# Values of two head pairs in one PSUM group, a lighter TensorE convolution in half the channel groups, and a planner that knows tiling switches

## The chip, the cores and the metric

One core of a Trainium2 chip runs the whole program. The metric is the device time of one execution in microseconds (us). "TensorE" or PE is the matmul engine, "VectorE" or DVE and "ScalarE" or ACT the two engines that read its results from PSUM here, POOL is GpSimd, SP issues the transfers.

## The reference

Banded attention (window of 32 to each side) for 8 batches, 8 heads, 576 positions and 64 channels a head; its output, as 576 x 512 per batch, goes through a gated FFN with a depthwise convolution of three taps.

```python
scores = np.where(abs(pos[:, None] - pos[None, :]) <= 32, q @ k.T / 8, -1e9)
x = softmax(scores) @ v                       # 8 x 576 x 512
h = np.maximum(x @ w_in, 0.0)                 # 8 x 576 x 1024
conv = sum(conv_w[k] * shifted(h, k - 1) for k in range(3))
out = (h * sigmoid(conv)) @ w_out             # 8 x 576 x 512
```

## The kernel before

The program declares each piece of work with its engine, an assumed duration and a priority. A planner (`place`) then fixes the order of all instructions and the PSUM banks (8 of 512 fp32 columns; bank pairs start at even banks). So an edit can move everything. The FFN runs in 12 blocks of 384 positions, each with 8 channel groups of 128. Attention for a later batch is woven between.

The convolution of one channel group: PE applies taps by multiplying with diagonal matrices, in blocks 0 and 1 all three, later only the outer two. VectorE then adds the middle tap in PSUM, ScalarE takes tanh, VectorE gates.

```python
def TAPS(c):
    return (0, 1, 2) if c < 2 else (0, 2)
...                                            # cut: in hidden(), for each group m
for kk in TAPS(c):
    nc.tensor.matmul(ps(sl, 0, no), diag_w[:, kk, m, :], hview(m, o0, o1, kk - 1),
                     start=(kk == 0), stop=(kk == 2))
...
if len(TAPS(c)) == 2:
    nc.vector.scalar_tensor_tensor(out=pv(), in0=mid, scalar=conv_w_sb[:, 1, m:m + 1],
                                   in1=pv(), op0=ALU.mult, op1=ALU.add)
```

The values step: for one pair of heads, 8 or 12 small matmuls (128x64 tiling of the array, 65 columns: 64 of values, one of row sums) into one bank, one reciprocal of the row sums, one multiply.

```python
def values(b, s, g, t):                        # cut
    sl = Slot(1)                               # one bank
    ...                                        # 4 * n matmuls of 64x65
    nc.vector.reciprocal(rv, view()[:, :, :, D])
    nc.vector.tensor_tensor(out=xn[...], in0=view()[:, :, :, 0:D], in1=rv..., op=ALU.mult)
...
for g in range(NP):                            # 4 pairs of heads
    values(b, s, g, ...)
```

Scores are in a third tiling (64x128), so PE's order switches between three modes. The planner before takes no account of that.

The softmax here doesn't subtract the row's maximum and nothing guards it: scores larger than these inputs give would overflow.

## Time and profile before

| | before |
|---|---|
| time, median of 4 runs | 237.56 us (236.97 to 238.3) |
| span of the profiled execution | 235.7 us |
| busy: PE, DVE, ACT, POOL | 94%, 72%, 76%, 66% |
| first matmul of FFN block 2, from the span's start | 62.6 us |
| from there to the end of PE's work ("the stretch") | 169.4 us |
| priced PE work in the stretch / PE standing still | 166.4 / 3.1 us |

The last rows come from PE's matmul starts in the trace.

### The profile page before, as it was taken

How to read it: one execution, taken by the hardware profiler on the slowest of the kernel's cores; microseconds unless marked ns; L12 is line 12 of the kernel's file. 1: busy time of each engine (PE TensorE's matmuls, PEld its weight loads, DVE VectorE, ACT ScalarE, POOL GpSimd, SP SyncE). 2: the span in 40 equal slices, each digit the busy share in tenths (PEclk: the TensorE clock that was granted, in tenths of full speed). 3: DMA queues.
4: the chain of work that ended last, by engine and by line, in shares of the span. 5: the costliest groups of instructions: out<-in, count | busy, mean ns of one | idle time of the engine just before them, and what ended most of it. 6: DMA issues, size and time to landing. Idle time of an engine off the chain costs nothing.

```text
span 235.7 us, 6684 instructions
## 1 busy us (share of the span) xinstructions
PE 222.7 (94%) x2556; PEld 134.6 (57%) x2556; DVE 169.1 (72%) x405; ACT 179.3 (76%) x360; POOL 154.8 (66%) x153
## 2 busy tenths in 40 slices
PE   3897999899989999999999999999999999999993
PEld 1455798758656555555565555655554655555541
DVE  7557777649599667867795957967887858956570
ACT  4689898959868877787969687888868876666652
POOL 3367885999999769697879669797988670000000
PEclk9999999999999999999999999999999999999999
DMA  5999999998875659997796969879989311421113
GB/s 161 248 334 322 274 281 284 315 263 272 202 179 148 172 152 263 236 168 211 202 216 168 293 163 261 244 185 243 240 246 155 87 56 44 104 89 44 65 71 133
DMA packets 68884, 45.93 MB, mean 195 GB/s; under 512 B 53980, under 2 KB 54004, under 8 KB 68852
## 3 DMA queue, kind: packets, MB, share of 16 engines
q1 hardware_dynamic: 68816, 45.50, 73.1%
q8 instruction: 20, 0.33, 0.6%
q14 instruction: 12, 0.10, 0.1%
q10 hardware_dynamic: 36, 0.01, 0.0%
HBM read 32.52 MB, written 9.44 MB: 178 GB/s over the span
## 4 chain that ended last, share of the span: by engine, by line
PE 65%; DMA 13%; SPq 6%; POOL 5%; DVE 3%; issue 3%; ACT 2%; ACTq 0%; POOLq 0%
PE ps_all L771 21%; PE ps_all L699 21%; PE ps_all L729 11%; DMA vst<-in_v_dram 7%; PE ps_all L570 5%; PE ps_all L478 4%; DMA wst<-in_moe_w_out_dram 4%; PE ps_all L528 3%; SPq L378 3%; DMA kst<-in_k_dram 2%; SPq L409 2%; SPq L601 1%; POOL vo L290 1%; POOL ve L290 1%; POOL w_out_sb L290 1%
## 5 line engine op out<-in xcount | busy, mean ns | idle before, releaser
L699 PE MATMUL ps_all<-xT,w_in_sb 128*128 128x385 bf16 (+4 forms) x448 | 78.6, 304 | 1.2 <-ACT xT L288 0.7
L771 PE MATMUL ps_all<-w_out_sb,gT 128*128 128x512 bf16 x288 | 67.4, 379 | 0.0
L751 DVE SCALAR_TENSOR_TENSOR gT<-ps_all,hT 128x384 bf16<-128x384 f32 (+3 forms) x112 | 53.8, 493 | 15.7 <-ACT ps_all L748 14.8
L744 DVE SCALAR_TENSOR_TENSOR ps_all<-hT,conv_w_sb,ps_all 128x384 f32<-128x384 bf16 x80 | 48.6, 616 | 20.1 <-PE ps_all L729 19.6
L552 POOL TENSOR_TENSOR attn<-attn,mask 128x1024 bf16<-128x1024 bf16 x24 | 50.8, 2133 | 12.0 <-ACT attn L541 11.1
L715 ACT ACTIVATE hT<-ps_all 128x385 bf16<-128x385 f32 (+4 forms) x112 | 49.7, 459 | 10.1 <-PE ps_all L699 9.5
L748 ACT ACTIVATE ps_all<-ps_all 128x384 f32<-128x384 f32 (+3 forms) x112 | 48.7, 450 | 10.5 <-DVE ps_all L744 8.4
L699 PEld LDWEIGHTS <-w_in_sb 128*128 128x128 bf16 x448 | 40.2, 98 | 21.7 <-issue 1.2
L729 PE MATMUL ps_all<-hT,diag_w 128*128 128x384 bf16 (+3 forms) x256 | 50.9, 297 | 0.2 <-ACT attn L541 0.2
L771 PEld LDWEIGHTS <-gT 128*128 128x128 bf16 x288 | 27.3, 98 | 29.5
L782 ACT COPY y<-ps_all 128x512 f32<-128x512 f32 x36 | 21.1, 590 | 24.9 <-PE ps_all L771 20.6
L541 ACT ACTIVATE attn<-ps_all 128x1024 bf16<-128x1024 f32 (+1 forms) x40 | 36.7, 943 | 0.3 <-PE ps_all L528 0.2
L290 POOL TENSOR_SCALAR vo<-vst 64x1024 bf16<-64x1024 f32 (+1 forms) x34 | 33.0, 971 | 4.0 <-DMA vst<-in_v_dram 1.4
L590 DVE TENSOR_TENSOR xn<-ps_all,rec 128x256 bf16<-128x256 f32 (+1 forms) x64 | 29.1, 484 | 0.3
L290 POOL TENSOR_SCALAR ve<-vst 128x512 bf16<-128x512 f32 (+1 forms) x39 | 24.3, 631 | 4.6 <-DMA vst<-in_v_dram 3.8
L290 POOL TENSOR_SCALAR kn<-kst 128x1152 bf16<-128x1152 f32 (+1 forms) x19 | 19.2, 1012 | 11.9 <-DMA kst<-in_k_dram 8.5
L729 PEld LDWEIGHTS <-diag_w 128*128 128x128 bf16 x256 | 21.2, 97 | 9.8 <-issue 0.3
L552 DVE TENSOR_TENSOR attn<-attn,mask 128x1024 bf16<-128x1024 bf16 (+1 forms) x16 | 15.0, 944 | 8.9 <-ACT attn L541 8.8
L570 PEld LDWEIGHTS <-attn 128*64 128x64 bf16 x640 | 13.3, 111 | 11.6 <-issue 9.2
L290 POOL TENSOR_SCALAR qn<-qst 128x1152 bf16<-128x1152 f32 (+1 forms) x18 | 18.7, 1045 | 0.7 <-PE ps_all L699 0.2
L570 PE MATMUL ps_all<-ve,attn 128*64 128x65 bf16 x384 | 17.4, 197 | 0.8 <-ACT hT L715 0.7
L288 ACT COPY qT<-ps_all 128x640 bf16<-128x640 bf16 (+1 forms) x24 | 17.4, 754 | 0.3
(50 smaller groups left out, 174.1 us busy)
## 6 DMA issues: line engine op xcount, KB each, us to landing
qst<-in_q_dram SPq DMA_DIRECT2D x32, 288.0 KB, 5.0
kst<-in_k_dram SPq DMA_DIRECT2D x32, 288.0 KB, 5.2
out_dram<-y SPq DMA_DIRECT2D x36, 256.0 KB, 3.0
vst<-in_v_dram SPq DMA_DIRECT2D x23, 256.0 KB, 6.1
vst<-in_v_dram SPq DMA_DIRECT2D x16, 192.0 KB, 5.6
wst<-in_moe_w_in_dram SPq DMA_DIRECT2D x2, 1024.0 KB, 7.6
wst<-in_moe_w_out_dram SPq DMA_DIRECT2D x2, 1024.0 KB, 8.9
xT<-xn SPq DMA_TRANSPOSE x30, 2.7
```

Source lines behind the costliest of these rows:

```text
L290: nc.gpsimd.tensor_scalar(out=out_, in0=in_, scalar1=1.0, scalar2=0.0, op0=ALU.mult, op1=ALU.add)
L541: add(act(2 * w), t + 0.1, lambda e: nc.scalar.activation(at, ps(sl, 0, 1024).rearrange("p (e x) -> p e x", e=2)[:, :, 0:w], AF.Exp, bias= ...
L552: lambda e: ENG[e].tensor_tensor(out=x_, in0=x_, in1=m_, op=ALU.mult),
L570: nc.tensor.matmul(ps(sl, (D + 1) * (n * h_ + x), (D + 1) * (n * h_ + x + 1), 64 * j, 64 * j + 64), attn[a][:, 512 * h_ + col:512 * h_ + c ...
L590: add(dve(2 * n * D), t + 0.1, lambda e: nc.vector.tensor_tensor(out=xn[i][:, cs[0]:cs[0] + n].rearrange("p c (e g) d -> p c e g d", e=2)[ ...
L699: nc.tensor.matmul(ps(sl, 0, n), w_in_sb[:, kc, m * 128:(m + 1) * 128], x_[:, kc, a0:a1], start=(kc == 0), stop=(kc == KC - 1),)
L715: nc.scalar.activation(o_, i_, AF.Relu, bias=0.0, scale=0.5)
L729: nc.tensor.matmul(ps(sl, 0, no), diag_w[:, kk, m, :], hview(m, o0, o1, kk - 1), start=(kk == 0), stop=(kk == 2),)
L744: add(("DVE", no / 960.0 + 0.13), tt + 0.1, lambda e, m=m, mid=mid, pv=pv: nc.vector.scalar_tensor_tensor(out=pv(), in0=mid, scalar=conv_w ...
L748: add(act(no), tt + 0.2, lambda e, sl=sl: nc.scalar.activation(ps(sl, 0, no), ps(sl, 0, no), AF.Tanh, bias=0.0, scale=1.0), writes=[sl], s ...
L751: add(dve(no), tt + 0.3, lambda e, m=m, mid=mid, i2=i2, pv=pv: nc.vector.scalar_tensor_tensor(out=gT[ig][:, m, o0:o1].rearrange("p (i x) - ...
L771: nc.tensor.matmul(ps(sl, 0, d_model), gT[ig][:, m, 128 * i:128 * i + 128], w_out_sb[:, m, :], start=(m == 0), stop=(m == MB - 1),)
```

## The change

The intent is to take work from PE, which is solid after the opening. Four channel groups of eight ("light") leave only the middle tap to PE, from block 2 on, and VectorE adds both outer taps. Values of two head pairs go through one two-bank group with one reciprocal. The planner charges 0.105 us for a switch of tiling and prefers to stay in a mode. All its times were tuned anew. Cut to its core:

```diff
-    def TAPS(c):
-        return (0, 1, 2) if c < 2 else (0, 2)
+    def taps(c, m):
+        if c < 2:
+            return TIMES["taps"][c]                       # (0, 1, 2)
+        return (1,) if m in TIMES["light"] else (0, 2)    # light: 1, 2, 3, 7
...
-            if len(TAPS(c)) == 2:
-                add(("DVE", no / 960.0 + 0.13), ...)      # middle tap
+            for kk in (0, 1, 2):
+                if kk in taps(c, m):
+                    continue
+                add(("DVE", no / 960.0 + 0.13), ...)      # each tap that PE left out
...
-    def values(b, s, g, t):
-        sl = Slot(1)
+    def values(b, s, g0, t):
+        sl = Slot(2)                                      # pairs g0 and g0 + 1
...
-        add(("DVE", 0.1), ..., reciprocal of 2 * n columns)
-        add(dve(2 * n * D), ..., multiply)
+        add(("DVE", 0.105), ..., reciprocal of 4 * n columns)
+        for y in range(2):
+            add(dve(2 * n * D), ..., multiply of half y)
...
-                key=lambda o: (o.prio, o.idx),
+                key=lambda o: (o.prio - stick[o.mode] * (o.mode == mode), o.idx),
             )
             s, f, e = opts[op]
+            if e == "PE" and op.mode != mode:
+                s = max(s, free[e] + self.SWITCH)         # 0.105 us
+                f = s + op.on[e]
...                                                       # cut: TIMES, a new draw of them all
```

More of the change, by code (lines that the diff above doesn't have):

```diff
@@ L19 @@
     "half": {
-        (0, 0): (27.75, 1.28),
-        (0, 1): (-3.95, 3.99),
-        (1, 0): (24.21, 2.64),
-        (1, 1): (46.04, 3.6),
-    },
-    "piece": [(-0.09, 1.6), (27.99, 0.33), (36.27, 0.86), (40.99, 2.81)],
-    "chunk": 56.82,
-    "step": 15.6,
-    "margin": 2.54,
-    "out": (15.31, 27.98, 29.58),
+        (0, 0): (31.5694, 1.811),
+        (0, 1): (-12.0798, 6.4258),
+        (1, 0): (10.8847, 1.1224),
+        (1, 1): (52.2414, 1.1441),
+    },
+    "piece": [(1.3474, 0.5492), (19.8197, 0.6478), (41.7976, 0.48), (37.8871, 3.3671)],
+    "chunk": 55.9707,
+    "step": 15.8076,
+    "margin": 4.0934,
+    "out": (22.7184, 23.9398, 32.491),
     "cast": {
-        "w_in": 11.95,
-        "w_out": 32.67,
+        "w_in": 6.0555,
+        "w_out": 19.2939,
     },
@@ L35 @@
         "qk00",
+        "qk01",
         "v00",
-        "qk01",
         "w_in1",
         "v01",
+        "w_out0",
         "w_in0",
         "qk10",
-        "w_out0",
         "v10",
-        "w_out1",
         "v11",
         "qk11",
+        "w_out1",
     ],
-    "ahead": (5.65, 4.52),
-    "cast_ahead": (11.32, 0.34),
-    "phase": (-0.13, 0.27, 0.32, 0.66, 0.67, -0.07, 1.2),
-    "lag": (2.21, 2.77, 2.38),
-    "flex": (3, 2),
-    "slack": (0.01, 0.03, 0.04, 0.49, 0.1),
-    "early": (0.0, 0.1, 0.0),
+    "ahead": (6.7067, 2.3146),
+    "cast_ahead": (7.3327, -5.381),
+    "phase": (-0.1226, 0.2243, 0.2305, 0.713, 0.4914, -0.0012, 1.0535),
+    "lag": (2.6148, 2.8913, 2.5401),
+    "flex": (4, 4),
+    "slack": (0.0, 0.1637, 0.0513, 0.1767, 0.3135),
+    "stick": (9.6288, 5.2177),
+    "taps": ((0, 1, 2), (0, 1, 2)),
+    "light": (1, 2, 3, 7),
+    "early": (0.0, 0.1095, 0.0438),
 }
@@ L62 @@
         "on", "run", "prio", "deps", "users", "left", "idx", "group", "alloc", "slots",
-        "lat", "dma", "start", "end", "eng", "rel",
+        "lat", "dma", "start", "end", "eng", "rel", "mode",
     )
@@ L87, in add @@
     def add(self, on, prio, run, reads=(), writes=(), alloc=None, slots=(), lat=None, dma=None,
-            group=None, rel=0.0):
+            group=None, rel=0.0, mode=0):
         op = Op()
@@ L93, in add @@
         op.start = op.end = op.eng = None
-        op.users, op.rel, op.group = [], rel, group
+        op.users, op.rel, op.group, op.mode = [], rel, group, mode
         deps = set()
@@ L114 @@
     LAT = {"PE": 0.22, "ACT": 0.16, "DVE": 0.13, "POOL": 0.2, "SP": 0.0, "ACTQ": 0.0}
+    SWITCH = 0.105
+    LATE = 0.07
     def place(self):
@@ L128, in place @@
         free = {"PE": 1.5, "ACT": 2.8, "DVE": 3.9, "POOL": 3.3, "SP": 0.8, "ACTQ": 0.8}
+        stick = (0.0,) + TIMES["stick"]
         early = dict(zip(("PE", "ACT", "DVE"), TIMES["early"]))
@@ L131, in place @@
         bank = [0.0] * (self.banks - 1) + [WARM[1]]
-        dma_free = 0.0
+        dma_free, mode = 0.0, 0
         cand = [op for op in self.ops if not op.left]
@@ L157, in place @@
                 for e, d in op.on.items():
+                    if e == "PE":
+                        r += self.LATE * (r > free[e])
                     s = max(r + early.get(e, 0.0) if r > 0.0 else r, free[e])
@@ L167, in place @@
                 (o for o in cand if opts[o][2] == e and opts[o][0] <= lim),
-                key=lambda o: (o.prio, o.idx),
+                key=lambda o: (o.prio - stick[o.mode] * (o.mode == mode), o.idx),
             )
             s, f, e = opts[op]
+            if e == "PE" and op.mode != mode:
+                s = max(s, free[e] + self.SWITCH)
+                f = s + op.on[e]
             op.start, op.eng = s, e
             free[e] = f
+            mode = op.mode if e == "PE" else mode
             if op.dma is not None:
@@ L244 @@
     NREC = 4
-    rec = [pp.tile([128, 8], FP32, name=f"rec{i}") for i in range(NREC)]
+    rec = [pp.tile([128, 12], FP32, name=f"rec{i}") for i in range(NREC)]
     xn = [pp.tile([128, NBLK, H, D], BF16, name=f"xn{i}") for i in range(NLD)]
@@ L278, in pe @@
     def pe(n, count=1):
-        return ("PE", count * (n / 2400.0 + 0.0025))
+        return ("PE", count * (n / 2400.0 + 0.003))
     def ps(slot, lo, hi, p0=0, p1=128):
@@ L537, in scores @@
             need += t_keys(0, i, 0) + t_keys(1, i, 0)
-        add(("PE", 0.018 * 2 * len(todo)), t, mm, reads=need, writes=[sl], alloc=sl, slots=[sl], group=gr)
+        add(("PE", 0.0146 * 2 * len(todo)), t, mm, reads=need, writes=[sl], alloc=sl, slots=[sl], group=gr, mode=1)
         at = attn[a].rearrange("p (e x) -> p e x", e=2)[:, :, 0:w]
@@ L558, in values @@
         n = len(cs)
-        sl = Slot(1)
+        sl = Slot(2)
         gr = []
         tiles = sorted({min(2 * c + j, NT - 1) for c in cs for j in range(2)})
-        src = {tt: where[b, g, tt] for tt in tiles}
+        src = {(g, tt): where[b, g, tt] for g in (g0, g0 + 1) for tt in tiles}
         def mm(e):
-            for h_ in range(2):
+            for y in range(2):
                 for x, c in enumerate(cs):
-                    for j in range(2):
-                        tt = min(2 * c + j, NT - 1)
-                        a, col = src[tt]
-                        nc.tensor.matmul(
-                            ps(sl, (D + 1) * (n * h_ + x), (D + 1) * (n * h_ + x + 1),
-                               64 * j, 64 * j + 64),
-                            attn[a][:, 512 * h_ + col:512 * h_ + col + 64],
-                            (vo if tt % 2 else ve)[i][:, tt // 2, g + NP * h_, :],
-                            start=True, stop=True,
-                        )
+                    for h_ in range(2):
+                        for j in range(2):
+                            tt = min(2 * c + j, NT - 1)
+                            a, col = src[g0 + y, tt]
+                            lo = 512 * y + (D + 1) * (2 * x + h_)
+                            nc.tensor.matmul(
+                                ps(sl, lo, lo + D + 1, 64 * j, 64 * j + 64),
+                                attn[a][:, 512 * h_ + col:512 * h_ + col + 64],
+                                (vo if tt % 2 else ve)[i][:, tt // 2, g0 + y + NP * h_, :],
+                                start=True, stop=True,
+                            )
@@ L578, in values @@
         need = [("ve", i, tt // 2, x) for tt in tiles if tt % 2 == 0 for x in range(2)]
         need += [("vo", i, tt // 2, x) for tt in tiles if tt % 2 for x in range(2)]
-        add(("PE", 0.02 * 4 * n), t, mm, reads=need + [("attn", a) for a in {a for a, _ in src.values()}],
-            writes=[sl], alloc=sl, slots=[sl], group=gr)
-        r = (2 * g + s) % NREC
-        def view():
-            return ps(sl, 0, 2 * n * (D + 1)).rearrange("p (e c x) -> p c e x", e=2, x=D + 1)
-        rv = rec[r][:, 0:2 * n].rearrange("p (c e) -> p c e", e=2)
@@ L588, in values @@
-        add(("DVE", 0.1), t + 0.1, lambda e: nc.vector.reciprocal(rv, view()[:, :, :, D]),
-            reads=[sl], writes=[("rec", r)], slots=[sl], group=gr)
-        add(dve(2 * n * D), t + 0.1, lambda e: nc.vector.tensor_tensor(
-            out=xn[i][:, cs[0]:cs[0] + n].rearrange("p c (e g) d -> p c e g d", e=2)[:, :, :, g],
-            in0=view()[:, :, :, 0:D], in1=rv.unsqueeze(3).broadcast_to([128, n, 2, D]), op=ALU.mult,
-        ), reads=[sl, ("rec", r)], writes=[("xn", i, c, g) for c in cs], slots=[sl], group=gr)
+        add(("PE", 0.016 * 8 * n), t, mm, reads=need + [("attn", a) for a in {a for a, _ in src.values()}],
+            writes=[sl], alloc=sl, slots=[sl], group=gr, mode=2)
@@ new lines, in values, with view @@
+        r = (g0 + s) % NREC
+        def view(y=None):
+            v_ = ps(sl, 0, 1024).rearrange("p (y z) -> p y z", y=2)[:, :, 0:2 * n * (D + 1)]
+            v_ = v_.rearrange("p y (r x) -> p y r x", x=D + 1)
+            return v_ if y is None else v_[:, y].rearrange("p (c e) x -> p c e x", e=2)
+        rv = rec[r][:, 0:4 * n].rearrange("p (y r) -> p y r", y=2)
+        add(("DVE", 0.105), t + 0.1, lambda e: nc.vector.reciprocal(rv, view()[:, :, :, D]),
+            reads=[sl], writes=[("rec", r)], slots=[sl], group=gr)
@@ new lines, in values @@
+        for y in range(2):
+            add(dve(2 * n * D), t + 0.1, lambda e, y=y: nc.vector.tensor_tensor(
+                out=xn[i][:, cs[0]:cs[0] + n].rearrange("p c (e g) d -> p c e g d", e=2)[:, :, :, g0 + y],
+                in0=view(y)[:, :, :, 0:D],
+                in1=rv[:, y].rearrange("p (c e) -> p c e", e=2).unsqueeze(3).broadcast_to([128, n, 2, D]),
+                op=ALU.mult,
+            ), reads=[sl, ("rec", r)], writes=[("xn", i, c, g0 + y) for c in cs], slots=[sl], group=gr)
@@ L645, in attention @@
                 scores(b, s, None, when(b, s, TIMES["phase"][3]))
-            for g in range(NP):
+            for g in range(0, NP, 2):
                 values(b, s, g, when(b, s, TIMES["phase"][4] + TIMES["phase"][5] * g))
@@ L727, in mm @@
             def mm(e, m=m, sl=sl):
-                for kk in TAPS(c):
+                ks = taps(c, m)
+                for kk in ks:
                     nc.tensor.matmul(
                         ps(sl, 0, no), diag_w[:, kk, m, :], hview(m, o0, o1, kk - 1),
-                        start=(kk == 0), stop=(kk == 2),
+                        start=(kk == ks[0]), stop=(kk == ks[-1]),
                     )
             tt = t + (m + TIMES["lag"][0]) * dt
-            add(pe(no, len(TAPS(c))), tt, mm, reads=hk + [("diag", kk, m) for kk in TAPS(c)], writes=[sl], alloc=sl,
+            add(pe(no, len(taps(c, m))), tt, mm, reads=hk + [("diag", kk, m) for kk in taps(c, m)], writes=[sl], alloc=sl,
                 slots=[sl], group=gr)
@@ L741, in pv @@
                 return ps(sl, 0, no).rearrange("p (i x) -> p i x", i=i2)
-            if len(TAPS(c)) == 2:
-                add(("DVE", no / 960.0 + 0.13), tt + 0.1, lambda e, m=m, mid=mid, pv=pv: nc.vector.scalar_tensor_tensor(
-                    out=pv(), in0=mid, scalar=conv_w_sb[:, 1, m:m + 1], in1=pv(),
+            for kk in (0, 1, 2):
+                if kk in taps(c, m):
+                    continue
+                add(("DVE", no / 960.0 + 0.13), tt + 0.1, lambda e, m=m, kk=kk, pv=pv: nc.vector.scalar_tensor_tensor(
+                    out=pv(), in0=hview(m, o0, o1, kk - 1), scalar=conv_w_sb[:, kk, m:m + 1], in1=pv(),
                     op0=ALU.mult, op1=ALU.add,
```

## The prediction

> **What bounds the kernel now.** I first read the busy shares and the slices over the span.
>
> ```profile
> span 235.7 us, 6684 instructions
> PE 222.7 (94%) x2556; PEld 134.6 (57%) x2556; DVE 169.1 (72%) x405; ACT 179.3 (76%) x360; POOL 154.8 (66%) x153
> PE   3897999899989999999999999999999999999993
> DVE  7557777649599667867795957967887858956570
> PEclk9999999999999999999999999999999999999999
> ```
>
> TensorE (PE) has a first stretch with gaps, then is solid to the last slice, at the full granted clock. No other engine is near its limit over any length. A busy PE need not be a full PE, so I next took the table of stretches, in which each row is a window and the first number after its length is PE's busy time, and after that the timeline of PE in one stretch.
>
> ```profile
> 0.00:20.00 20.00, 13.94 (x164) 8.12 (x165) 12.41 (x56) 13.77 (x19) 9.46 (x19) 1.00 0.98 244
> 20.00:40.00 20.00, 19.31 (x297) 16.18 (x297) 14.53 (x40) 18.76 (x56) 15.43 (x23) 1.00 1.02 292
> ...
> 120.00:140.00 20.00, 20.00 (x239) 11.71 (x237) 14.98 (x34) 15.14 (x28) 14.70 (x14) 1.00 0.77 190
> 140.00:160.00 20.00, 20.00 (x220) 11.19 (x220) 15.09 (x34) 16.09 (x32) 17.58 (x15) 1.00 0.92 237
> ```
>
> ```profile
> 126.57 0.41 PE L528 MATMUL ps_all<-qT,kT 64*128 64x64 bf16 x16
> 126.91 0.50 PE L729 MATMUL ps_all<-hT,diag_w 128*128 128x384 bf16 x2
> 127.25 0.82 PE L699 MATMUL ps_all<-xT,w_in_sb 128*128 128x385 bf16 x4
> 127.90 0.49 PE L729 MATMUL ps_all<-hT,diag_w 128*128 128x384 bf16 x2
> 128.23 0.82 PE L699 MATMUL ps_all<-xT,w_in_sb 128*128 128x385 bf16 x4
> 128.98 0.22 PE L570 MATMUL ps_all<-ve,attn 128*64 128x65 bf16 x1
> ```
>
> Here starts matter, not durations. Two conv matmuls take 127.90 to 128.23 = 0.33 us, 0.163 each. Four first-layer matmuls followed by conv take 127.25 to 127.90 = 0.65 us; the same four followed by the values matmuls (128x64 tiling) take 128.23 to 128.98 = 0.75. So a change of tiling costs 0.10 us going in. Over the whole trace the median start-to-start steps are 0.216 us for 512 columns (0.309 when a values matmul follows), 0.163 for 384, 0.056 for 128, about 0.016 per matmul within scores or values, and 0.122 to 0.128 for the last of these before a full-array matmul. Both ways cost about 0.10 us.
>
> With these steps I priced every matmul in the built program's PE order. The sum is 210.0 us. By trace time the first 20 us hold only 4.9 us of such work and 20 to 60 us hold 36.4: the opening waits for loads, casts and the first attention chain. FFN block 2, the first with the cheaper convolution, starts at 62.6 us; from there to PE's end at 232.0 us pass 169.4 us, and the work in them is 166.3. PE therefore stands still about 3 us in the last 170. It is the bound there, and a PE microsecond removed there can become one of span.
>
> **What the Trainium skill says.**
> "TensorEngine Tiling (Array Packing)", Key Properties: changing the tiling mode drains the TensorE. The trace agrees, at about 0.10 us per change.
> "TensorE: Matmul & The Clock Gate", Back-to-back issue gap: N/2.4 + 2.5 ns alone, but about 131 ns per N=512 matmul in a stream with weight loads. The first form fits (163 and 216 ns); the second does not, as the 288 output matmuls step at 216 ns. I use the trace.
> "PSUM — Partial Sum Buffer", Specifications: a VectorE instruction may take one tensor input from PSUM. The extra taps respect this: the shifted hidden values lie in SBUF, the partial sum in PSUM.
> "Perfetto Trace Analysis", Optimizing Scalar/DVE Operations: a fixed cost per DVE instruction of some 60 ns on SBUF and 125 ns on PSUM, so grouping helps a saturated engine. Steps of 0.530 us for the 384-element tap (0.400 is 384 elements at 0.96 GHz) and of 0.11 us for a reciprocal of 4 or 6 elements agree with the second figure.
>
> **The change, part by part.**
> Taps: blocks 0 and 1 keep three PE taps. In blocks 2 to 11, channel groups 1, 2, 3 and 7 now put one tap instead of two on PE. That is 10 x 4 = 40 matmuls fewer; the build has 216 conv matmuls instead of 256. 40 x 0.163 = 6.5 us of PE, all after 62 us. VectorE (DVE) gets 40 more of this row:
>
> ```profile
> L744 DVE SCALAR_TENSOR_TENSOR ps_all<-hT,conv_w_sb,ps_all 128x384 f32<-128x384 bf16 x80 | 48.6, 616 | 20.1 <-PE ps_all L729 19.6
> L751 DVE SCALAR_TENSOR_TENSOR gT<-ps_all,hT 128x384 bf16<-128x384 f32 x80 | 43.3, 551 | 12.4 <-ACT ps_all L748 11.8
> L588 DVE RECIPROCAL rec<-ps_all 128x6 f32<-128x6 f32 x32 | 5.2, 183 | 2.2 <-PE ps_all L570 2.2
> ```
>
> 40 x 0.53 = 21.2 us when the next instruction overlaps the end of one. The build puts the two taps of a group mostly next to each other, and the second needs the first. A dependent pair of reciprocal and multiply steps at duration plus 0.04 us in the trace, so a tap followed by its partner takes 0.616 + 0.04 = 0.66: up to 40 x 0.13 = 5 us more.
>
> Values: the matmuls are the same 640. 32 of 64 reciprocals go, 32 x 0.11 = 3.5 us of DVE; the multiplies remain. Each group now holds two banks, from its first matmul to its second multiply.
>
> Switches: in PE's order the mode changes fall from 131 to 97, so 34 x 0.10 = 3.4 us; by block, some 3.0 of it lies from block 2 on and the rest in the opening.
>
> PE's priced sum is thus 200.1 instead of 210.0, from block 2 on 156.8 instead of 166.3 (9.5 us less), in the opening 0.4 less. The load order is nearly the old one, but the second half of batch 0's q and k now precedes its first v loads, and five more opening casts are on POOL instead of ScalarE, 0.62 to 0.67 us each. POOL at 66% of the span can take them, but the first v casts come later. I charge +0.5 us there; that is judgment.
>
> What takes back: DVE's steps in blocks 2 to 9 sum to 112 us, against 126.7 us of PE. With the dependent pairs it is about 117, so 92%, where before it was 96 against 134.7 (72%). Blocks 10 and 11 are easy (20 against 30). At 92%, in strict order, DVE will sometimes be late with a bank or with the normalised rows that feed the transposes. I charge 2.5 us of new PE waits, nearly doubling the 3 us of now. That is the least certain term.
>
> Sum: 237.9 - 9.9 + 0.5 + 2.5 = 231.0 us, 2.9% less.
>
> **The rivals.**
> First, DVE becomes the bound. For: 92% in the middle, and block 7 has 15.3 us of DVE steps against 15.0 of PE. Against: the loads average out over blocks, and much of DVE's idle time now is waiting for PE's own conv result (19.6 us in the row above), not for work that came too late. It would put 5 to 8 us of waits on PE: 234 to 236, within 2%.
> Second, PSUM pressure. Value groups take an even-aligned pair of banks, like scores, and a light conv bank waits for one more DVE step of about 0.6 us. If PE then waits for banks, it shows as waits on DVE or ACT ahead of score, value or first-layer matmuls: 2 to 5 us, so 232 to 235. Against: PE's waits for banks are few now.
> Third, everything removed is worth its price and the new order also packs the opening better, since switching less often lets it run longer bursts: 227 to 229.
> Fourth, the opening gets slower by 2 us or more because casts of v queue on POOL: 232 to 234.
>
> **Range and chances.** The middle is the sum; half the charge for waits up or down, and an opening off by 1 us either way, give 229 to 233. The first rival in full and the third set the ends: 227.5 to 235.0. Faster by over 2% means below 233.1, which fails if new waits and the opening exceed 5.1 us in all: one chance in four. Slower than 242.6 would need the whole gain lost and as much again in waits; I give it 2%.
>
> **What would show each step.** Right: conv matmuls 216, DVE tap rows 120 at about 616 ns, DVE busy some 20 us more (near 80% of a shorter span), 32 reciprocals, the PE step into and out of values still 0.10 us; block 2 starts within 1 us of 62.6; from there to PE's end about 162 us (156.8 and 5.5 of waits). Wrong: PE waits on DVE totalling over 5 us after 62 us, or DVE solid in the middle slices with PE in eights (first rival); waits for freed banks ahead of values and scores (second); block 2 starting after 64.5 us (fourth). If the extra tap steps take far longer than 0.62 us because of the shifted reads, the DVE sum and with it the whole middle is wrong.

## More of the kernel before

"Priced work" is the sum of steady start-to-start steps as the prediction works them out, and what the stretch is longer than this is PE standing still. The prediction shows the views that this rests on.

## The result, and the profile after

The changed kernel takes **231.28 us** (230.8 to 232.35, 4 runs), against 237.56. The ratio is 0.974 (95% interval 0.969 to 0.979). Ratios here are the mean time of one kernel's fast runs over that of the other's of the same rounds, so they are not quite the ratios of the quoted medians. The predicted 231.0 us was met; not all of its terms were.

The first lines of the page of the kernel after, to hold against those in the prediction:

```profile
span 228.8 us, 6559 instructions
PE 213.2 (93%) x2519; PEld 130.9 (57%) x2519; DVE 191.7 (84%) x416; ACT 170.8 (75%) x350; POOL 160.2 (70%) x160
PE   3785999999999997999999998999999999999992
DVE  6966576977989889988899989998898988998780
PEclk9998899999999999999999999999999999999999
```

PE is still solid once the opening is over, in a shorter span. DVE has gone up by 22.6 us, and in the middle its slices read eight and nine where they read six and seven. The table of stretches, first at the same two windows as in the prediction and then DVE alone:

```profile
0.00:20.00 20.00, 11.60 (x145) 6.51 (x147) 15.42 (x50) 9.93 (x13) 13.75 (x24) 1.00 0.95 231
20.00:40.00 20.00, 19.47 (x295) 15.97 (x289) 12.33 (x33) 16.22 (x49) 17.33 (x26) 0.91 1.11 317
...
120.00:140.00 20.00, 20.00 (x221) 11.41 (x218) 17.99 (x36) 17.12 (x33) 17.30 (x15) 1.00 1.01 224
140.00:160.00 20.00, 19.29 (x250) 11.51 (x249) 19.00 (x39) 15.60 (x29) 16.08 (x15) 1.00 0.72 196
```

The columns are PE, weight loads, DVE, ACT and POOL. In the first 20 us PE is busy less than before (11.6 us against 13.9), ACT too (9.9 against 13.8), POOL more (13.75 against 9.46); the granted clock falls to 0.91 of full in the next window. From 80 to 200 us, adding up such rows, DVE is busy 109.7 of 120 us (91%), before 91.6 (76%).

The groups that the change touches:

```profile
L768 DVE SCALAR_TENSOR_TENSOR ps_all<-hT,conv_w_sb,ps_all 128x384 f32<-128x384 bf16 x120 | 70.8, 615 | 6.6 <-PE ps_all L751 5.2
L775 DVE SCALAR_TENSOR_TENSOR gT<-ps_all,hT 128x384 bf16<-128x384 f32 x80 | 42.7, 549 | 3.9 <-ACT ps_all L772 2.9
L605 DVE RECIPROCAL rec<-ps_all 128x12 f32<-128x12 f32 x16 | 3.5, 221 | 3.2 <-PE ps_all L586 3.1
L605 DVE RECIPROCAL rec<-ps_all 128x8 f32<-128x8 f32 x16 | 3.3, 205 | 2.8 <-PE ps_all L586 2.6
```

120 taps at 615 ns each, as in the 80 of before at 616: the shifted reads cost nothing extra. What DVE used to wait for PE's convolution (19.6 us) is now 5.2 us. In the starts of the trace a tap that is followed by an independent instruction steps at 0.525 us, one followed directly by its own partner at about 0.65 us (18 of the 40 pairs).

PE's waits from 62 us on, the view of who waited for whom (total us, times, longest; it lists waits over 0.15 us):

```profile
PE ps_all L586 <- DVE attn L565: 1.9, 2, 1.2
PE ps_all L630 <- DVE xT L307: 0.2, 1, 0.2
PE ps_all L491 <- POOL kn L303: 0.2, 1, 0.2
```

The largest is the values matmuls waiting for masked scores: by start-to-start steps these two waits cost 2.4 of the 3.9 us that PE stands still. The second line is at 62.9 us, before the stretch: transposes that wait for a copy out of PSUM, which frees a bank. In the stretch no line is a wait for a bank; the list of weight loads, which come ahead of their matmuls, has one, a convolution at 66.2 us released by a gating multiply, of which PE lost some 0.2 us. Where the time went, from the two traces:

| part of the span | before | after | difference | priced work in it |
|---|---|---|---|---|
| start to block 2 | 62.6 | 64.0 | +1.4 | -0.4 |
| block 2 to PE's end | 169.4 | 160.8 | -8.7 | -9.5 |
| PE's end to the span's end | 3.7 | 4.1 | +0.4 | 0 |
| span | 235.7 | 228.8 | -6.9 | -9.9 |

So the stretch kept 8.7 of 9.5 us (PE stands still 3.9 us instead of 3.1), and the opening and the close gave back 1.8. These are two single executions; between the medians the gain is 6.3 us, not 6.9.

### The profile page after: what moved, and what is told of

Same layout as the page of the kernel before. It is cut to its first block, busy times and chain, and to the rows that moved or that the text cites. A ratio compares the mean times of both kernels' runs of the same rounds, so it can differ in the third digit from the quotient of the medians.

```text
span 228.8 us, 6559 instructions
## 1 busy us (share of the span) xinstructions
PE 213.2 (93%) x2519; PEld 130.9 (57%) x2519; DVE 191.7 (84%) x416; ACT 170.8 (75%) x350; POOL 160.2 (70%) x160
## 4 chain that ended last, share of the span: by engine, by line
PE 64%; POOL 18%; DMA 7%; DVE 4%; issue 2%; SPq 2%; ACT 0%; ACTq 0%; POOLq 0%
PE ps_all L720 22%; PE ps_all L795 21%; PE ps_all L751 9%; POOL vo L303 4%; PE ps_all L586 4%; PE ps_all L491 4%; POOL ve L303 4%; POOL attn L565 4%; DMA wst<-in_moe_w_out_dram 3%; DMA vst<-in_v_dram 3%; PE ps_all L541 3%; POOL w_out_sb L303 2%; SPq L391 2%; POOL qn L303 2%; POOL kn L303 2%
## 5 line engine op out<-in xcount | busy, mean ns | idle before, releaser
L768 DVE SCALAR_TENSOR_TENSOR ps_all<-hT,conv_w_sb,ps_all 128x384 f32<-128x384 bf16 x120 | 70.8, 615 | 6.6 <-PE ps_all L751 5.2
L736 ACT ACTIVATE hT<-ps_all 128x385 bf16<-128x385 f32 (+4 forms) x112 | 48.5, 461 | 11.7 <-PE ps_all L720 10.7
L751 PE MATMUL ps_all<-hT,diag_w 128*128 128x384 bf16 (+3 forms) x216 | 43.3, 291 | 0.2
L303 POOL TENSOR_SCALAR vo<-vst 64x1024 bf16<-64x1024 f32 (+1 forms) x36 | 35.4, 982 | 2.9
L303 POOL TENSOR_SCALAR ve<-vst 128x512 bf16<-128x512 f32 (+1 forms) x41 | 26.6, 661 | 2.4 <-DMA vst<-in_v_dram 1.5
L608 DVE TENSOR_TENSOR xn<-ps_all,rec 128x256 bf16<-128x256 f32 (+1 forms) x64 | 27.9, 481 | 0.3
L751 PEld LDWEIGHTS <-diag_w 128*128 128x128 bf16 x216 | 18.2, 97 | 7.7 <-DVE gT L775 0.5
L565 DVE TENSOR_TENSOR attn<-attn,mask 128x1024 bf16<-128x1024 bf16 (+1 forms) x16 | 16.3, 1037 | 2.7 <-ACT attn L554 2.6
L586 PE MATMUL ps_all<-ve,attn 128*64 128x65 bf16 x384 | 15.6, 197 | 1.9 <-DVE attn L565 1.9
L586 PE MATMUL ps_all<-vo,attn 128*64 128x65 bf16 x256 | 14.5, 197 | 2.7 <-POOL vo L303 2.7
```

The lines of the kernel that those rows point to most:

```text
L303: nc.gpsimd.tensor_scalar(out=out_, in0=in_, scalar1=1.0, scalar2=0.0, op0=ALU.mult, op1=ALU.add)
L565: lambda e: ENG[e].tensor_tensor(out=x_, in0=x_, in1=m_, op=ALU.mult),
L586: nc.tensor.matmul(ps(sl, lo, lo + D + 1, 64 * j, 64 * j + 64), attn[a][:, 512 * h_ + col:512 * h_ + col + 64], (vo if tt % 2 else ve)[i][ ...
L608: add(dve(2 * n * D), t + 0.1, lambda e, y=y: nc.vector.tensor_tensor(out=xn[i][:, cs[0]:cs[0] + n].rearrange("p c (e g) d -> p c e g d", ...
L736: nc.scalar.activation(o_, i_, AF.Relu, bias=0.0, scale=0.5)
L768: add(("DVE", no / 960.0 + 0.13), tt + 0.1, lambda e, m=m, kk=kk, pv=pv: nc.vector.scalar_tensor_tensor(out=pv(), in0=hview(m, o0, o1, kk ...
```

## The experiments

Twelve kernels ran, four to a chip, all beside the kernel before. For each, the "stretch" is read from its profiled execution. Its priced work is taken from the built program, because a few traces lack some matmul records (pe_tap_back has 2534 of 2559). Unless said, results were correct.

| kernel | time, us | ratio to before (95%) | block 2 at | stretch | priced work | PE stands still |
|---|---|---|---|---|---|---|
| before | 237.6 | | 62.6 | 169.4 | 166.4 | 3.1 |
| after | 231.3 | 0.974 (0.969 to 0.979) | 64.0 | 160.8 | 156.9 | 3.9 |
| pe_tap_back | 234.7 | 0.985 (0.981 to 0.990) | 63.9 | 165.3 | 163.4 | 1.9 |
| switch_in_values | 236.6 | 0.993 (0.987 to 0.998) | 66.4 | 164.9 | 161.9 | 3.0 |
| same_mode_in_values | 231.5 | 0.974 (0.968 to 0.979) | 64.7 | 160.6 | 157.5 | 3.1 |
| short_second_tap | 230.6 | 0.970 (0.965 to 0.974) | 65.2 | 159.9 | 156.9 | 3.0 |
| no_light | 235.5 | 0.991 (0.987 to 0.995) | 63.2 | 165.9 | 163.1 | 2.9 |
| six_light | 232.5 | 0.978 (0.975 to 0.981) | 65.3 | 162.6 | 154.4 | 8.2 |
| blind_planner | 235.8 | 0.993 (0.987 to 0.998) | 65.6 | 163.9 | 158.0 | 5.9 |
| small_replan | 233.0 | 0.981 (0.978 to 0.985) | 63.9 | 162.9 | 157.7 | 5.3 |
| single_values | 241.8 (3 fast runs) | 1.014 (1.008 to 1.021) | profile slow | | | |
| casts_to_act | 231.4 | 0.975 (0.969 to 0.980) | 65.4 | 161.4 | 156.9 | 4.5 |
| mask_from_psum | 230.6 | 0.972 (0.966 to 0.977) | 64.2 | 160.9 | 156.9 | 4.0 |
| act_casts_psum_mask | 230.3 | 0.969 (0.964 to 0.973) | 64.3 | 160.7 | 156.9 | 3.8 |

Seven of them keep the planned order of instructions and change only what is issued. The other five are planned anew, which turned out to matter.

### What a microsecond of PE is worth: pe_tap_back

```diff
                 ks = taps(c, m)
+                if len(ks) == 1:                 # overwritten by the next matmul
+                    nc.tensor.matmul(ps(sl, 0, no), diag_w[:, 0, m, :],
+                                     hview(m, o0, o1, -1), start=True, stop=True)
                 for kk in ks:
```

> The changed kernel with its order of instructions kept; each of the 40 light conv blocks also issues, ahead of its one real tap, a second 128x384 matmul into the same bank, which the real one overwrites (right result). VectorE's work is unchanged, so this prices the TensorE time that the change removed. My theory (TensorE still bounds the stretch from block 2 on): 40 x 0.163 = 6.5 us more work gives back 5 to 6.5 us, so 236 to 238 against 231.3. Rival (VectorE, at 92% in the middle, has become the bound): the extra matmuls fit in TensorE's new waits and the time grows by at most 2 us, to 233.

234.7 us: the ratio rises from 0.974 to 0.985, about 2.6 us by ratios and 3.4 by medians. In the trace the stretch grows by 4.5 of the 6.5 us put in, and PE stands still 2.0 us less. This lies between the two expectations. In the stretch about two thirds of the PE time becomes time, in the medians half of it; the rest was already lost to waits that the lighter PE runs into.

### What a switch costs: switch_in_values and its control

```diff
             for y in range(2):
+                if y == 1:      # switch_in_values: full array, 128 x 64 columns
+                    nc.tensor.matmul(ps(sl, 448, 512), ident, mask_[:, 0:64], start=True, stop=True)
+                    # same_mode_in_values instead: 128x64 tiling, as the values are
+                    nc.tensor.matmul(ps(sl, 448, 512, 0, 64), ident[:, 0:64], mask_[:, 0:64], ...)
```

> The changed kernel with its order kept; between the two halves of each of the 32 values groups one small full-array matmul (64 columns into unused columns of the bank) is issued, so the tiling mode goes out and back 32 times more. 64 switches at 0.10 us are 6.4 us, of which 44 (4.4 us) fall from block 2 on, where TensorE is the bound; the matmuls themselves add some 0.03 us each, 0.7 us there. My theory: 5 us more than the changed kernel, 236 to 237. Rival (a switch overlaps with waits, or its 0.10 us is only the first matmul's latency): within 1.5 us of the control that stays in the mode.

> Control for the run with switches inside values: the same 32 small matmuls at the same places, but in the 128x64 tiling of the values themselves, so no switch is added. My theory: 22 of them from block 2 on at 0.02 to 0.03 us, so within 0.7 us of the changed kernel, 231 to 232, and 4 us or more faster than its partner. Rival: the same as its partner.

The control is the changed kernel within the error (231.5, ratio 0.974). The partner takes 236.6, 5.1 us more on the same chip. In the stretch, 164.9 against 160.6 us is 4.25 us for 44 switches, 0.097 us each; in the opening 1.7 us for 20, though block 2's start also scatters by itself (see casts_to_act). PE's timeline in the kernel with switches shows one pair of them: the full-array matmul is the line with 128x64 bf16 and tiling 128*128.

```profile
120.36 0.23 PE L588 MATMUL ps_all<-ve,attn 128*64 128x65 bf16 x4
120.52 0.20 PE L581 MATMUL ps_all<-mask,ident 128*128 128x64 bf16 x1
120.65 0.22 PE L588 MATMUL ps_all<-ve,attn 128*64 128x65 bf16 x1
```

From the lone matmul to the next values matmul pass 0.13 us, for work of 0.03 us. Over the trace, the step from the last values matmul to the inserted one is 0.128 us with a switch and 0.030 without. The price of a switch is real time on PE and is shown.

### Does VectorE's load make the waits: short_second_tap

```diff
-                    out=pv(), in0=hview(m, o0, o1, kk - 1), ...
+                    out=cut(pv(), m, kk), in0=cut(hview(m, o0, o1, kk - 1), m, kk), ...
+            def cut(v_, m, kk):                  # wrong result on purpose
+                return v_[:, :, 0:8] if kk == 2 and len(taps(c, m)) == 1 else v_
```

> The changed kernel with its order kept, but in the light conv blocks the second VectorE tap covers 8 columns instead of 384 (wrong result on purpose). This takes away some 40 x 0.4 = 16 us of VectorE work and leaves TensorE's as it is. In the changed kernel TensorE stands still 3.7 us from block 2 on. My theory (VectorE's load costs only part of these waits): 0.5 to 2.5 us faster than 231.3, so 229 to 231. Rival (VectorE is what limits the middle): 4 us or more faster, below 227.5.

230.6 us, ratio 0.970 against 0.974, with intervals that overlap; the stretch is 0.9 us shorter. Taking 16 us of work from an engine that is 91% busy in the middle gains about a microsecond; the intervals would allow some 2.5, but not the rival's 4. At four light groups VectorE is close to its limit but does not set the pace.

### More and fewer light groups: no_light and six_light

```diff
-    "light": (1, 2, 3, 7),
+    "light": (),                       # no_light
+    "light": (0, 1, 2, 3, 5, 7),       # six_light
```

> The changed kernel without the light blocks: two taps on TensorE and one on VectorE everywhere from block 2 on, as before; the plan is made anew, so the order moves. TensorE's priced work from block 2 on is 163.1 us against 156.9. My theory: 5 to 6 us slower than the changed kernel, 236 to 237.5, nearly as slow as the kernel before. Rival (the switches and pairs carry most of the gain, and VectorE's relief makes up for the taps): 231 to 233.

> The changed kernel with six of eight channel groups light instead of four. TensorE's priced work from block 2 on falls by 2.5 us to 154.4 (switches rise to 105), VectorE's rises by 20 x 0.53 to 0.66 = 11 to 13 us, past TensorE's in blocks 2 to 9 (about 127 against 124). My theory: here VectorE becomes the bound and the time rises by 2 to 6 us, 233 to 237. Rival (VectorE has room left because the load averages over blocks): 229 to 231.

Without light groups the time is 235.5 us, a little under the range expected, and the stretch is 5.2 us longer than in the changed kernel. Compared with the kernel before (169.4), its stretch is 3.5 us shorter, with 29 switches fewer there (63 against 92, 2.9 us at 0.10). So the stretch's gain of 8.7 us parts into about 3.5 for values and planner and 5.2 for the taps, as the priced work says (3.3 and 6.2). But a new plan has a price of its own: the control small_replan, below, lengthens the stretch by 2.1 us with no change of the work that is asked for. Against that control, which is planned anew too, the stretch without light groups is 3.0 us longer and the time some 2.3 us (0.991 against 0.981), so the light groups are worth between 2.3 and 4.0 us.

With six, PE has 2.5 us less work than with four, and stands still 4.3 us more. 232.5 us is just under the range of my theory and above that of the rival. The windows show where VectorE has nothing left, here DVE from 200 to 224 us, where no attention is left, in the kernels after and with six light groups:

```profile
200.00:224.00 24.00, 19.74 (x37) 1.00 0.17 66
```

```profile
200.00:224.00 24.00, 23.73 (x47) 1.00 0.21 78
```

With six, DVE is full in the last blocks, which I had called easy for four. So six are no gain over the tuned plan with four. Against small_replan (0.981) they are no loss either (0.978, the intervals overlap): whether six would gain under times tuned for them was not tested.

### The planner: blind_planner, single_values, and the control small_replan

```diff
-    SWITCH = 0.105                     # blind_planner: 0.0
-    LATE = 0.07                        # 0.0
-    "stick": (9.6288, 5.2177),         # (0.0, 0.0)
...
+    def values(b, s, g, t): ...        # single_values: one pair, one bank, as before
...
-    "step": 15.8076, "margin": 4.0934, # small_replan: 15.83, 4.05
```

> The changed kernel with the planner's three additions at zero (cost of a switch, the lateness of a waiting TensorE, the preference for staying in a mode); pairs and light blocks stay. Switches 111 instead of 97, priced work from block 2 on 158.0 instead of 156.9 us. My theory: pairing alone gives most of the fall in switches and knowing them is worth some 1 to 2 us, so 232 to 233.5. Rival (the knowledge itself carries the gain, since the plan and the chip drift apart without it): 235 or more.

> The changed kernel with values of one head pair per one-bank group again (64 groups, 64 reciprocals), the planner still knowing switches; the plan is made anew. Switches 120 instead of 97, TensorE's priced work from block 2 on 158.4 instead of 156.9 us, VectorE 32 x 0.11 to 0.12 us more. My theory: 1.5 to 3 us slower, 233 to 234. Rival (a pair of banks held longer costs more than the switches give): the same or faster, 230 to 231.5.

> Control for the runs whose plan was made anew (no light blocks, single values, blind planner, six light): the changed kernel with two planner times moved a little (step 15.8076 to 15.83, margin 4.0934 to 4.05), nothing else. If the times are tuned to this one plan, a new plan by itself costs 1 to 3 us, 232 to 234, and differences of that size in those four runs say nothing of their edits. If not, within 0.7 us of 231.3.

The control decides how these may be read. Moving two planner times by 0.14% and 1% costs 1.8 us by ratios (0.981 against 0.974): 8 switches more in the stretch, and PE stands still 1.4 us longer. The new times fit this one plan.

blind_planner is at 235.8 us, in the rival's range. Of the 4.5 us over the changed kernel (by medians), some 1.8 may be the price of a new plan, as far as one control tells. Its stretch holds 1.1 us more priced work (11 switches) and 2.0 us more standing still, little more than small_replan's 1.4. How much of the rest is the missing knowledge and how much its opening (block 2 at 65.6) these runs do not settle.

single_values missed both expectations: 241.8 us, slower than the kernel before, with fast runs between 239.5 and 242.6. Its profiled run was slow, so its trace is not compared; in it block 2 started only at 73.4 us, which is where one would look first, but a slow run shows no cause. Its priced work is only 1.5 us above the changed kernel's, so switches are not the reason. The new times were tuned with pairs. What pairing is worth by itself stays open. The static counts are 131 switches before, 120 with the planner's knowledge and single values, 111 with pairs and a blind planner, 97 with both.

### The opening: casts_to_act

In the changed kernel the first FFN matmul starts at 23.9 us, 2.6 us later than before. POOL's timeline there:

```profile
13.43 0.62 POOL L303 TENSOR_SCALAR ve<-vst 128x512 bf16<-128x512 f32 x1 [0.50 <-DMA vst<-in_v_dram]
14.13 1.07 POOL L303 TENSOR_SCALAR vo<-vst 64x512 bf16<-64x512 f32 x1
15.29 1.64 POOL L303 TENSOR_SCALAR ve<-vst 128x512 bf16<-128x512 f32 x2
17.01 2.70 POOL L303 TENSOR_SCALAR vo<-vst 64x512 bf16<-64x512 f32 x3
```

```diff
     order = plan.place()
+    for op in moved:        # of batch 0's first v rows, one plain and two shifted casts
+        op.eng = "ACT"
```

> The changed kernel with its order kept, but three of the seven casts of batch 0's first v rows run on ScalarE again, which is idle there (9.9 of the first 20 us busy). In the changed kernel the seven stand one after the other on POOL from 13.4 to 19.7 us, the first FFN matmul waits for them and starts at 23.9 us (21.2 before), and block 2 at 64.0 (62.6 before). Theory (the casts on POOL are what the opening lost): first FFN matmul at 21.5 to 22.5 us, block 2 0.7 to 1.5 us earlier, 230 to 230.7 in all. Rival (the loads set block 2's start, the casts only the first matmul's): first matmul earlier, block 2 and the time unchanged within 0.4 us.

231.4 us, no change; the first FFN matmul came at 24.3 us in its profiled run and block 2 at 65.4. The theory fell in this form. On ACT the casts stood among the exponentials, and PE then waited for one of those and for a cast there:

```profile
18.18 0.19 PE L592 MATMUL ps_all<-ve,attn 128*64 128x65 bf16 x1 [0.39 <-ACT attn L560]
19.65 0.22 PE L592 MATMUL ps_all<-vo,attn 128*64 128x65 bf16 x1 [1.21 <-ACT vo L301]
```

The fall of the clock at 20 to 25 us is not the reason for the late block 2 either: the same order in pe_tap_back kept the full clock there and reached block 2 at 63.9, against 64.0. That leaves the order of loads (the second half of q and k ahead of the first v) as a cause that was not tested. And the 1.4 us are themselves uncertain: five kernels whose order up to block 2 is that of the changed kernel, or nearly (after, pe_tap_back, mask_from_psum, same_mode_in_values, short_second_tap), start it between 63.9 and 65.2, and the kernel before has one trace. What costs the opening its time is open.

### Two engines at one port: mask_from_psum

PE's largest wait in the stretch, 1.2 us, ends with a mask multiply on VectorE. DVE's and then POOL's timeline in the kernel after, at that time, and DVE's at the last such multiply, when POOL has nothing left to do:

```profile
88.51 2.19 DVE L565 TENSOR_TENSOR attn<-attn,mask 128x512 bf16<-128x512 bf16 x1
90.63 0.55 DVE L775 SCALAR_TENSOR_TENSOR gT<-ps_all,hT 128x384 bf16<-128x384 f32 x1
```

```profile
86.22 4.21 POOL L565 TENSOR_TENSOR attn<-attn,mask 128x1024 bf16<-128x1024 bf16 x2
90.39 1.33 POOL L303 TENSOR_SCALAR kn<-kst 128x1152 bf16<-128x1152 f32 x1
```

```profile
187.85 0.42 DVE L565 TENSOR_TENSOR attn<-attn,mask 128x512 bf16<-128x512 bf16 x1
```

The same instruction takes 0.42 us alone and 2.19 us when it meets POOL's, and it ends 0.3 us after POOL's second multiply (88.30 to 90.42). The other long one, 1.80 us at 139.2, ends 0.3 us after a POOL multiply as well. The Trainium skill, "SBUF — State Buffer", section "SBUF: two separate sides", says that VectorE and GpSimd share one port pair under an exclusive lock, which an instruction with two SBUF inputs takes too, against a GpSimd instruction that reads SBUF. To test it, the multiply was given one input in PSUM:

```diff
-            at, ps(sl, 0, 1024)..., AF.Exp, ...
+            pw() if late else at, pw(), AF.Exp, ...       # late: last score tile, batches 2 to 7
...
-            lambda e: ENG[e].tensor_tensor(out=x_, in0=x_, in1=m_, op=ALU.mult),
+            lambda e: ENG[e].tensor_tensor(out=x_, in0=pw()... if late else x_, in1=m_, op=ALU.mult),
```

> The changed kernel with its order kept; for batches 2 to 7 the exponential of the last score tile (128x512) stays in PSUM, and VectorE's mask multiply reads it there, so that this instruction has one input in SBUF instead of two. In the changed kernel's trace this multiply takes 0.42 us with POOL idle but 2.20 and 1.80 us when it meets a POOL mask multiply, ending just after that one does, and TensorE then waits 1.2 and 0.7 us for it. Theory (the two engines exclude each other when both read two SBUF tensors): the six multiplies take 0.65 to 0.75 us each, TensorE's waits for this row go, 1 to 2 us in all, so 229.3 to 230.5. Rival (the multiply is slow for another reason, or the waits are only passed on to another operand): durations of 1 us and more remain, or the time stays within 0.4 us of 231.3.

The result was wrong, by an oversight: the plan counts the banks as free after the exponential, and in one of the six cases it gives them to two other matmul groups ahead of the multiply. The durations still tell. The group of these multiplies in this kernel:

```profile
L569 DVE TENSOR_TENSOR attn<-ps_all,mask 128x512 bf16<-128x512 f32 x6 | 4.1, 684 | 0.5 <-ACT ps_all L777 0.5
```

All six took 0.68 to 0.69 us, three of them inside a POOL mask multiply (one at 89.07, with POOL's from 88.54 to 90.68). So the lock is shown, and with one SBUF input the instruction passes it. PE's wait for this row is gone. The gain did not follow: the stretch is 160.9 against 160.8 us, the other waits grew, and the ratio of 0.972 has an interval that holds 0.974.

### Both: act_casts_psum_mask

> Both of the above in one kernel, the candidate that should beat both kernels: if the opening and the middle are separate, their gains add, 228.5 to 230; if POOL's full stretch from 40 to 90 us is what really sets the pace of the opening and the first blocks, it is no better than the better one of the two.

230.3 us, ratio 0.969 (0.964 to 0.973), with the same wrong result. Its interval overlaps that of the changed kernel, and in its profile the stretch is 160.7 us. It can't be called better, and no correct version here beats the changed kernel.

## Why the prediction was right, point by point

**What bounds the kernel.** PE, from block 2 on: right. Matmuls put back lengthen the time by 2.6 to 3.4 us for 6.5 (the stretch by 4.5), less than the 5 I expected at least, so the bound is not a full one; switches put in, within the stretch, by nearly their whole price (4.25 us of 4.4).

**The priced work, 9.5 us less in the stretch.** Right. 216 conv matmuls, 97 switches, steps of 0.163 us and about 0.10 us hold in the trace, and the switch also by experiment (0.097). One part was misread: from block 2 on the switches fall from 92 to 66, so by 2.6 us and not 3.0. The sum stands, because three convolution matmuls of an early block and eight score matmuls moved ahead of block 2.

**VectorE's side.** Right: 120 taps at 615 ns, dependent pairs at 0.65 (0.66 expected), though only 18 of 40 follow directly and not most of them; 91% busy in the middle (92% expected, but counted by steps, which gave 72% before where busy time gives 76%), +22.6 us busy ("some 20"). The reciprocals of 8 and 12 step at 0.12 and 0.14 us, not 0.11, which makes some 0.6 us in all.

**New PE waits, +2.5 us.** Too large by a factor of three: +0.8. A VectorE at 91% did not delay PE as I charged: short_second_tap shows that its second taps cost about a microsecond. I had no measure for waits of an engine at such a load and guessed. But the charge is hidden in the price of the taps too: pe_tap_back finds 2.0 us of waits that come with the lighter PE.

**The opening, +0.5 us (with 0.4 less work).** Too small: +1.4. And the close, which I left out, +0.4. I named the order of loads and the casts on POOL as the reasons; moving three casts back did nothing, and the loads were not tested, so the reasons I gave are not confirmed.

So that 231.0 comes so near to 231.3 is in part luck: two misses of opposite sign, 1.7 us too much in the waits and 1.7 too little at both ends. The sum also started from 237.9, one run's time; from the median of 237.56 the kernel fell by 6.3 us where 6.9 were forecast.

**The rivals.** VectorE as the bound is refuted for four light groups; at six it fills the last blocks. PSUM pressure hardly shows: of PE's waits in the stretch only some 0.2 us is seen to be for a freed bank. "Everything is worth its price" was nearest for the stretch (8.7 of 9.5). A slower opening came, at two thirds of the size that the rival named.

## What to carry to other kernels

Price the bounding engine by start-to-start steps in the trace, per form of instruction and per change of mode, and check the sum against the stretch; then the most that a change is worth on that engine can be added up from the program's order alone; new waits take back a part, here a third of the taps' price. Work moved to a second engine was nearly free here while that engine had room in every stretch, and its average does not show that: four light groups of eight were worth 2.3 to 4.0 us of the time, and with six DVE was full in the last blocks. When a planner is tuned to one plan, run a small, meaningless change of it as a control before reading anything from variants that are planned anew: here it cost 1.8 us.

## What the Trainium skill lacked or had wrong

- "TensorEngine Tiling (Array Packing)", Key Properties, says that a mode switch drains the array but gives no cost. Here it is 0.09 to 0.11 us (0.309 against 0.216 us after a 512-column matmul; 0.097 us each when 44 were put in).
- "TensorE: Matmul & The Clock Gate", Back-to-back issue gap, gives about 131 ns per N=512 matmul in a stream with weight loads. Here 256 such steps have a median of 216 ns, before and after, as its form for a single gap gives.
- "Perfetto Trace Analysis", Optimizing Scalar/DVE Operations: some 125 ns fixed cost on PSUM fits the taps, which read and write PSUM (0.525 to 0.530 us for 0.400 of elements: multiplies of 384 and 256 elements step at 0.465 and 0.331, so 1.05 ns an element), but not the gating instruction, which reads PSUM and writes SBUF: 0.467 us, so 67 ns. The reciprocals of the kernel before, also from PSUM to SBUF, lie between: 0.100 and 0.112 us for 4 and 6 elements, so some 0.10 fixed, and not quite the agreement that the prediction read into them.
- "SBUF — State Buffer", SBUF: two separate sides, is right on the lock, and other parts of the page also give the way out, at most one input in SBUF. What it lacks is the price of that: with one of the two inputs in PSUM the multiply took 0.68 to 0.69 us in six of six cases, three of them beside a POOL multiply, instead of 0.42 alone and up to 2.19 when it has to wait.
- No page states as a figure the cost of an immediate dependence on VectorE: a tap followed by the one that needs it steps at 0.65 us instead of 0.525.
